# Empty rows stored two steps later, off the scatters' path, and a shorter plan for each expert slot

## The chip, the cores and the metric

One core of a Trainium2 chip runs the whole program. The metric is device time in microseconds (us) of that core; the median of three runs of the kernel before is 650.07 us (649.31 to 651.37).

## The reference

Windowed attention feeds a mixture of experts (MoE). There are 8 batches, 8 heads, 576 positions and head width 64; the 4608 rows that come out have 512 columns and go through one of 8 experts each, with hidden width 1024.

```python
scores = scale * np.matmul(q, k.transpose(0, 1, 3, 2))
mask = (rel >= 0) & (rel < window)                 # window = 64
attn = softmax(np.where(mask, scores, -1e9))
x = (attn @ v).transpose(0, 2, 1, 3).reshape(N, 512)
logits = x @ w_gate + modality_bias[modality_id]
e_idx = np.argmax(logits, axis=1)
gate_w = softmax(logits)[np.arange(N), e_idx]
for e in range(E):
    mask = e_idx == e
    out[mask] = gate_w[mask, None] * (np.maximum(x[mask] @ w1[e], 0.0) @ w2[e])
```

## The kernel before, in words

**Attention steps.** The 4608 rows are 36 pairs of 64-row blocks, 128 rows each. The main loop runs over steps `s` from 0 to 39. In step `s` the program takes the scores and minima of pair `s` (`scores`, `minima`, `exps`), transposes the probabilities of pair `s-1` (`probs_t`; ACT copies them out of PSUM as `pT`, L622) and multiplies by the values of pair `s-2` (`values`, PE tile `av`, L639). `values` needs `ve`, a copy of the pair's value rows shifted by half a pair, made one step earlier in `swap_v`: its lower half by POOL (L515), its upper half by DVE (L514). The result `xa` (L647) is transposed and goes to the gate logits of pair `s-3` (L664). The order on every engine is the order in which the code is written: instructions of an engine wait for their inputs in line.

**Routing.** Every two pairs form a group `G`. In step `s = 2G+5` a small matmul counts, for each row, the rows before it with the same expert (`route2`); `route3` makes from it the row's place `idx` in a DRAM table `xs_scratch`, and two indirect DMAs on POOL (L740, "scatters", one for each pair) store the 514-word rows (x, gate, row number) there. `cnt`, the eight experts' counts so far, comes out of PSUM at L765 where it is needed. The routing operations of DVE wait in a list `routing`, other small table operations in a list `queue`; `tick(n)` issues up to n of them, first the routing's, and with `table=True` the queue's.

**Empty rows.** Each expert's rows in the table are filled up with empty rows, whose row number is out of range. The table's last 256 rows are such empty rows; they are stored from the tile `padrow` by one DMA on SP's queue (L1065, in the profile `xs_scratch<-xt`, 514 KB) at the end of step 4. A step's scatters start in step 5.

**Expert slots.** From step 12 (`FIRST`) on, PE's work of expert slots is mixed into the attention steps: a slot takes 256 rows of one expert, loads them (`load_slot`, tile `xt`, L205), and runs both layers with split weights (`first` L283, `second` L305). The weights of two experts, 0 and 1 of `sel2`, stay in SBUF; their pieces come from DRAM as `y` tiles (L100, L104) during the attention steps, POOL casts the high part (L111) before step 12, and DVE makes the low part (L118). Table `EARLY` lists ten groups `T` behind whose scatters a slot is planned. `plan` computes which rows the slot reads: the number of full 256-row tiles of the expert counted so far, less those used, at most one; if there is none, the empty rows. SP reads the row number into a register (L203) and issues the load. After the attention steps the remaining tiles are planned and run by PE alone.

```python
        n = per_expert(pl, nm + "_n", tiles_of(pl, nm + "_f", cnt, False, TP), xs_)   # 3 + 2 operations
        n = tt(pl, nm + "_av", n, used[-1][:, xs_], ALU.subtract)
        take = ts(pl, nm + "_take", n, 1.0, ALU.min)
        row = stt(pl, nm + "_first", used[-1][:, xs_], 2.0, base2[:, xs_], ALU.mult, ALU.add)
        row = tt(pl, nm + "_at", row, take, ALU.mult)
        rows = ts(tab, f"rows_{len(used)}", row, float(DUMMY), ALU.add, dtype=I32)
        # and one or two more for the new number of used tiles: 11 or 12 in all
```

The first plan (`T` = 2) is written at the end of step 9; its 12 operations are issued in step 10 (`table`), and step 11 fetches the slot.

## Time and profile before

| | |
|---|---|
| median of the runs | 650.07 us (649.31 to 651.37) |
| the profiled execution | 651.72 us, of which the span of instructions 649.9 us |
| PE (matmul) busy | 621.9 us, 96% of the span |
| DVE, ACT, POOL busy | 366.5, 298.9, 139.9 us |
| mean granted TensorE clock | 0.985 |
| DMA | 88.59 MB, mean 136 GB/s |

Busy shares are means over stages with different limits, so the stretches have to be read one by one: the start and the first twelve steps last until about 91 us, then attention steps and slots run together, and after about 360 us slots alone. In the profile a wait is put down to the instruction that ended last before it, which need not be the one that was waited for.

### The profile page before, as it was taken

The page shows a single profiled execution, that of the slowest core. Times are in us where ns is not written, and L with a number is a line of the kernel's source. Part 1 is how long each engine was busy: PE and PEld are TensorE (multiplying, and loading weights), DVE is VectorE, ACT ScalarE, POOL GpSimd, SP SyncE. Part 2 cuts the span into 40 slices and gives each one's busy share as a digit, 9 for nine tenths or more (in the row PEclk, how much of TensorE's full clock was granted, in tenths as well). Part 3 has the DMA queues.
Part 4 walks back from the last instruction along what each step waited for, and adds up shares of the span by engine and source line. Part 5 has one row for each costly group of instructions (what it writes and reads, how often), then busy time and mean ns, then how long its engine had stood idle before and what let it go on. Part 6 is the DMA issues. An engine that isn't in the chain of part 4 may idle for free. (4 is left out here: it accounts for less than half of the span.)

```text
span 649.9 us, 17274 instructions
## 1 busy us (share of the span) xinstructions
PE 621.9 (96%) x6508; PEld 558.9 (86%) x6509; DVE 366.5 (56%) x1487; ACT 298.9 (46%) x931; POOL 139.9 (22%) x322
## 2 busy tenths in 40 slices
PE   6887889999999999999999999999999999999996
PEld 4777778988898989888888989999899999989986
DVE  2975996777767775766654364122223634757611
ACT  3875866756565656555644111111113422555411
POOL 5313530222132122221322220011011101101102
PEclk9996989999999999999999999999999999999999
DMA  9989675766855755453322123511050642677300
GB/s 166 197 217 223 174 203 136 189 159 149 195 139 130 186 138 136 108 133 88 99 84 66 66 98 129 198 66 56 15 189 34 215 142 80 212 246 234 119 2 35
DMA packets 140965, 88.59 MB, mean 136 GB/s; under 512 B 118826, under 2 KB 118864, under 8 KB 140752
## 3 DMA queue, kind: packets, MB, share of 16 engines
q1 hardware_dynamic: 132192, 67.97, 41.8%
q0 software_dynamic: 5856, 18.92, 7.7%
q10 hardware_dynamic: 2832, 0.59, 0.7%
q8 instruction: 52, 0.85, 0.6%
q14 instruction: 33, 0.27, 0.2%
HBM read 68.01 MB, written 23.91 MB: 141 GB/s over the span
## 5 line engine op out<-in xcount | busy, mean ns | idle before, releaser
L305 PE MATMUL y<-Whi,hh 128*128 128x512 f32 x288 | 118.7, 412 | 0.0
L305 PE MATMUL y<-Whi,hl 128*128 128x512 f32 x288 | 113.0, 392 | 0.0
L305 PE MATMUL y<-Wlo,hh 128*128 128x512 f32 x288 | 112.7, 391 | 0.0
L283 PE MATMUL em<-xh,Whi 128*128 128x256 f32 x400 | 102.7, 291 | 1.0 <-DVE xl L195 1.0
L283 PE MATMUL em<-xh,Wlo 128*128 128x256 f32 x400 | 98.0, 279 | 0.0
L613 ACT ACTIVATE ss<-ss,mn 128x128 f32<-128x128 f32 x240 | 94.1, 398 | 4.1 <-DVE mn L601 4.1
L292 DVE SCALAR_TENSOR_TENSOR hl<-em,hh 128x512 fp32r<-128x512 f32 x50 | 34.5, 690 | 94.2 <-ACT hh L291 92.5
L316 POOL DMA_INDIRECT out_dram<-y,id x36 | 37.3, 1036 | 224.1 <-DVE y L313 144.9
L283 PEld LDWEIGHTS em<-xh,Whi 128*128 128x128 f32 x400 | 75.3, 188 | 2.2 <-DVE xl L195 1.3
L283 PEld LDWEIGHTS em<-xh,Wlo 128*128 128x128 f32 x400 | 75.4, 188 | 0.9
L291 ACT ACTIVATE hh<-em 128x512 fp32r<-128x512 f32 x50 | 29.6, 593 | 92.9 <-PE em L283 88.9
L622 ACT COPY pT<-tp 128x512 f32<-128x512 f32 x59 | 32.7, 589 | 75.6 <-PE tp L443 75.6
L305 PEld LDWEIGHTS y<-Whi,hl 128*128 128x128 f32 x288 | 54.0, 188 | 12.3
L601 DVE CUSTOM_DVE_ANT_0 ss<-sp,masks 128x128 f32<-128x128 f32 x240 | 53.6, 286 | 19.1 <-PE sp L584 18.7
L283 PE MATMUL em<-xl,Whi 128*128 128x256 f32 x400 | 63.0, 279 | 0.0
L305 PEld LDWEIGHTS y<-Wlo,hh 128*128 128x128 f32 x288 | 54.3, 189 | 7.2
L305 PEld LDWEIGHTS y<-Whi,hh 128*128 128x128 f32 x288 | 54.1, 188 | 7.4
L740 POOL DMA_INDIRECT xs_scratch<-xa,idx x36 | 36.2, 1007 | 88.9 <-DVE lm L683 26.0
L639 PEld LDWEIGHTS av<-ve,pT 128*64 128x64 f32 x576 | 37.8, 142 | 19.5 <-POOL ve L515 9.3
L283 PEld LDWEIGHTS em<-xl,Whi 128*128 128x128 f32 x400 | 53.7, 188 | 0.0
L639 PE MATMUL av<-ve,pT 128*64 128x64 f32 x576 | 42.8, 230 | 10.0 <-POOL ve L515 6.3
L292 DVE SCALAR_TENSOR_TENSOR hl<-sp,hh 128x512 fp32r<-128x512 f32 x22 | 15.2, 691 | 61.1 <-ACT hh L291 61.1
(261 smaller groups left out, 1298.0 us busy)
## 6 DMA issues: line engine op xcount, KB each, us to landing
xt<-xs_scratch SPq DMA_DIRECT2D x18, 514.0 KB, 3.9
y<-in_moe_w_dram SPq DMA_DIRECT2D x32, 256.0 KB, 4.2
vo<-in_v_dram SPq DMA_DIRECT2D x27, 256.0 KB, 3.0
vo<-in_moe_w_dram SPq DMA_DIRECT2D x24, 256.0 KB, 4.0
ss<-in_moe_w_dram SPq DMA_DIRECT2D x24, 256.0 KB, 3.6
xs_scratch<-xs_scratch SPq DMA_DIRECT2D x8, 514.0 KB, 5.6
qk<-in_q_dram SPq DMA_DIRECT2D x16, 256.0 KB, 4.9
qk<-in_k_dram SPq DMA_DIRECT2D x16, 256.0 KB, 5.9
```

The source lines that it names most:

```text
L283: nc.tensor.matmul(out=hb[:, i * TP:(i + 1) * TP], lhsT=w[buf][:, c0:c0 + P], rhs=x[:, c * TP:(c + 1) * TP], start=(n == 0), stop=(n == le ...
L291: nc.scalar.activation(out=hh, in_=hb, func=AF.Relu),
L292: nc.vector.scalar_tensor_tensor(out=hl, in0=hb, scalar=0.0, in1=hh.bitcast(F32), op0=ALU.max, op1=ALU.subtract)))
L305: nc.tensor.matmul(out=sl["y", t], lhsT=h[:, i * TP + t * P:i * TP + (t + 1) * P], rhs=w[buf][:, c0:c0 + DM], start=(k == 0 and n == 0), s ...
L316: ins = nc.gpsimd.indirect_dma_start(out=out, out_offset=bass.IndirectOffsetOnAxis(ap=sl["id"][:, t:t + 1], axis=0), in_=y, in_offset=None ...
L601: nc.vector.tensor_tensor_reduce(out=ss[a][:, hp, :], in0=sp[a][:, hp * P:(hp + 1) * P], in1=mask, scale=-1.0 / 8.0, scalar=3.0e38, op0=AL ...
L613: nc.scalar.activation(out=ss[a][:, hp, :], in_=ss[a][:, hp, :], func=AF.Exp, bias=mn[:, h:h + 1], scale=-1.0, accum_out=sm[:, h:h + 1])
L622: nc.scalar.copy(out=pT, in_=pp)
L639: nc.tensor.matmul(out=av[c * W64:(c + 1) * W64, 2 * hp + a], lhsT=pT[:, i:i + W64], rhs=(vo if c else ve)[p][:, 2 * hp + a, :], start=Tru ...
L740: ins = nc.gpsimd.indirect_dma_start(out=xs, out_offset=bass.IndirectOffsetOnAxis(ap=idx[:, j:j + 1], axis=0), in_=xg[j], in_offset=None)
```

## The change

1. The store of the empty rows moves from the end of step 4 to the end of step 6, and is declared free of the scatters (their rows are never the same).
2. The plan of a slot keeps running numbers for each of the two experts: `used2`, `row2` (the expert's next row, in place of `base2`) and `room2` (the count from which a further full tile is there, 256 at first). A slot is taken where the expert's count is at least `room2`, so the counts need not be turned into tiles. 8 operations of DVE stand where 11 or 12 stood; four of them (five where two slots are planned) lead to the row number, the others carry the numbers on. A slot waits for the former alone (`need`).
3. The plan is written right behind the counts, ahead of `route3`, not at the end of the step. For the first plan (step 9) six operations are issued there at once; `table` for step 10 is gone.

```diff
+        n = per_expert(pl, nm + "_n", cnt, xs_)
+        used, row, room = used2[:, xs_], row2[:, xs_], room2[:, xs_]
+        one = xs_.stop - xs_.start < 2
+        if one:
+            at = stt(pl, nm + "_at", n, room, row, ALU.is_ge, ALU.mult)
+        else:
+            take = tt(pl, nm + "_take", n, room, ALU.is_ge)
+            at = tt(pl, nm + "_at", row, take, ALU.mult)
+        rows = ts(tab, f"rows_{len(todo)}_{T}", at, float(DUMMY), ALU.add, dtype=I32)
+        need = queued()
+        if one:
+            take = tt(pl, nm + "_take", n, room, ALU.is_ge)
+        tt(pl, nm, used, take, ALU.add, out=used)
+        stt(pl, nm, take, 2.0, row, ALU.mult, ALU.add, out=row)
+        stt(pl, nm, take, float(TP), room, ALU.mult, ALU.add, out=room)
...
-        table = s == FIRST - 2
...
-        tick(6 if table else 2, table)
+        tick(2)
...
-        tick(8 if table else n_tick, table)
+        tick(n_tick)
...
                 cnt = counts_out(tab if R == NG - 1 else pl, counts(R, tp))
+            for T, xs_ in EARLY:
+                if T == R:
+                    plan(T, xs_, cnt)
+                    tick(6 if s < FIRST else 0, table=True)
             route3(R, rk)
...
-        if s == 4:
-            nc.sync.dma_start(out=xs_blk[DUMMY:DUMMY + 2].rearrange("b p c -> p b c"), in_=padrow)
-        for T, xs_ in EARLY:
-            if T == R:
-                plan(T, xs_, cnt)
+        if s == 6:
+            ins = nc.sync.dma_start(out=xs_blk[DUMMY:DUMMY + 2].rearrange("b p c -> p b c"), in_=padrow)
+            tc.declare_no_dep(ins.ins, group="scatter", reason="rows behind every token's row")
+            tc.add_to_no_dep_group("scatter", ins.ins)
```

Three places of the built programs show what moved. POOL in step 5, at the first two scatters (`xa<-idc` writes the row numbers; the names in brackets are what the instruction waits for, DMAHW being DMAs of SP's queue):

```order
 L628 TENSOR_SCALAR rs<-sm 128x8 [waits DVE_49,Activation_49]
 L739 COPY xa_101<-idc 128x1
-L740 DMA xs_scratch<-xa_101,idx 39168x514 [waits DMAHW1_49,DVE_49,Pool_49]
+L740 DMA xs_scratch<-xa_101,idx 39168x514 [waits DVE_49,Pool_49]
 L739 COPY xa_102<-idc 128x1
 L740 DMA xs_scratch<-xa_102,idx 39168x514 [waits Pool_49]
```

The first scatter no longer waits for the DMA of the empty rows; nothing else on POOL moved. SP's queue in steps 4 to 7, before (`y` are weight pieces, `vo` values, the `Wlo` tiles hold q and k of later groups):

```order
L100 DMA y<-in_moe_w_dram 128x512
L1065 DMA xs_scratch<-xt 128x2x514
L536 DMA Wlo_65<-in_k_dram 128x8x64 x2
L100 ISA
L100 DMA y<-in_moe_w_dram 128x512
L501 DMA vo<-in_v_dram 128x8x64
```

and after, from the last piece of step 6 on:

```order
L104 ISA
L104 DMA y<-in_moe_w_dram 128x512
L1070 DMA xs_scratch<-xt 128x2x514
L501 DMA vo<-in_v_dram 128x8x64
L536 DMA Wlo_65<-in_k_dram 96x8x64 x2
```

The store goes past two weight pieces, one value load and six loads of k and q, and now stands ahead of the values of pair 7. DVE in step 10 before, behind the upper half of `ve` (the last of the 12 operations, `e_used`, follows):

```order
L514 COPY ve<-vo 64x512
L141 TENSOR_SCALAR e_f_i<-cnt 1x8
L165 TENSOR_SCALAR e_f_s<-e_f_i 1x8
L141 TENSOR_SCALAR e_f<-e_f_s 1x8
L153 TENSOR_TENSOR e_n_p<-sel_68,e_f 1x8
L158 TENSOR_REDUCE e_n<-e_n_p 1x1
L153 TENSOR_TENSOR e_av<-e_n,used_216 1x1
L550 COPY kT<-em 128x2x2x128
L141 TENSOR_SCALAR e_take<-e_av 1x1
L147 SCALAR_TENSOR_TENSOR e_first<-used_216,base_69 1x1
L153 TENSOR_TENSOR e_at<-e_first,e_take 1x1
L141 TENSOR_SCALAR rows_1495<-e_at 1x1
```

and DVE in step 9 after, behind the counts:

```order
L765 COPY cnt<-tp 1x8
L153 TENSOR_TENSOR e_n_p<-sel_68,cnt 1x8
L158 TENSOR_REDUCE e_n<-e_n_p 1x1
L147 SCALAR_TENSOR_TENSOR e_at<-e_n,room_226,row_69 1x1
L141 TENSOR_SCALAR rows_2_1462<-e_at 1x1
L153 TENSOR_TENSOR e_take<-e_n,room_226 1x1
L153 TENSOR_TENSOR used_216<-used_216,e_take 1x1
L721 TENSOR_TENSOR tgt<-tp,ebase 128x16
```

Six operations of the plan now stand ahead of the routing of step 9 (`tgt` is its first operation), and two, for `row2` and `room2`, behind the routing of step 10.

## The prediction

> **What bounds the kernel now.** I read the busy times by stretches first (columns: stretch, its length, busy us and instructions of PE, weight loads, DVE, ACT, POOL, then granted clock, DMA share, GB/s), and then PE's waits.

> ```profile
> 42.00:66.00 24.00, 18.25 (x280) 16.82 (x281) 14.53 (x70) 14.75 (x59) 8.19 (x15) 0.72 0.97 230
> 66.00:92.00 26.00, 21.73 (x415) 19.58 (x411) 24.32 (x131) 20.98 (x83) 11.13 (x21) 0.93 0.72 192
> 112.00:330.00 218.00, 216.33 (x2843) 194.89 (x2838) 151.27 (x732) 127.71 (x449) 53.66 (x110) 1.00 0.57 142
> 330.00:640.00 310.00, 309.50 (x2196) 279.37 (x2195) 133.15 (x333) 93.03 (x188) 44.06 (x97) 1.00 0.35 117
> ...
> PE av L639 <- POOL ve L515: 5.8, 2, 3.6
> ...
> PE em L443 <- DVE xa L647: 1.9, 1, 1.9
> PE av L639 <- DVE e_f_i L141: 1.2, 1, 1.2
> ```

> From 112 us on PE is full (216.33 of 218, 309.50 of 310), with the DMA engines half busy: what is lost or won before 112 us shifts everything behind it, and nothing there can take it up. Before that no engine is full. From 42 to 66 us PE waits 5.8 us for POOL's `ve` and its clock is 0.72; from 66 to 92 us DVE is busy 24.32 of 26. The change touches both places.

> Third, POOL's timeline at the first scatters, with the rows of SP, DVE and PE that belong to it (start, length, what, and in brackets the idle time before):

> ```profile
> 43.98 0.61 POOL L515 COPY ve<-Wlo 64x512 f32<-64x512 f32 x1
> 45.28 0.19 POOL L739 COPY xa<-idc 128x1 f32<-128x1 f32 x1
> 50.94 1.21 POOL L740 DMA_INDIRECT xs_scratch<-xa,idx  x1 [5.47 <-DVE lg L684]
> 52.17 0.19 POOL L739 COPY xa<-idc 128x1 f32<-128x1 f32 x1
> 52.64 0.96 POOL L740 DMA_INDIRECT xs_scratch<-xa,idx  x1 [0.28 <-POOL xa L739]
> 53.60 0.63 POOL L111 CAST Whi<-y 128x512 fp32r<-128x512 f32 x1
> 54.15 0.62 POOL L515 COPY ve<-Wlo 64x512 f32<-64x512 f32 x1
> ...
> 44.98 0.43 SPq L1065 DMA_DIRECT2D xs_scratch<-xt  x1
> ...
> 43.35 0.15 DVE L752 CAST idx<-dst 128x2 int32<-128x2 f32 x1
> 50.67 0.18 DVE L684 TENSOR_TENSOR lg<-lg,lm 128x16 f32<-128x16 f32 x1
> ...
> 50.66 0.60 PE L443 MATMUL em<-ident_r,Whi 128*128 128x128 f32 x4
> 54.83 0.37 PE L639 MATMUL av<-ve,pT 128*64 128x64 f32 x1 [3.57 <-POOL ve L515]
> ```

> The scatter's places `idx` are ready at 43.50 us (43.35 + 0.15), its row numbers at 45.47; it starts at 50.94. The profile names DVE `lg` only because that ended last before; the scatter does not read it. What it waits for is the empty rows' DMA, issued at 44.98. Behind it in POOL's line stand the second scatter, a weight cast and the `ve` that PE needs at 51.26 (50.66 + 0.60): PE stands until 54.83.

> Fourth, the clock in the same places (stretches cut where it changes), and ACT's first `pT` copy of each of steps 6 to 9, the beat of the steps:

> ```profile
> 43.08:46.49 3.41, 1.85 (x59) 1.83 (x62) 2.29 (x9) 3.16 (x14) 1.91 (x4) 1.00 1.04 250
> 46.49:49.91 3.42, 3.42 (x42) 3.09 (x35) 1.96 (x18) 0.59 (x2) 0.00 (x0) 0.50 1.10 286
> 49.91:53.32 3.41, 1.35 (x12) 1.12 (x10) 2.14 (x10) 3.41 (x16) 2.08 (x3) 1.00 0.99 235
> 53.32:63.56 10.24, 8.73 (x102) 8.32 (x103) 4.77 (x22) 4.07 (x16) 3.62 (x8) 0.50 1.11 244
> ...
> 49.05 0.59 ACT L622 COPY pT<-y 128x512 f32<-128x512 f32 x1 [2.81 <-PE y L443]
> 49.91 0.59 ACT L622 COPY pT<-y 128x512 f32<-128x512 f32 x1 [0.27 <-PE y L443]
> 60.56 0.59 ACT L622 COPY pT<-y 128x512 f32<-128x512 f32 x1 [5.91 <-PE y L443]
> 67.06 0.59 ACT L622 COPY pT<-tp 128x512 f32<-128x512 f32 x1 [0.97 <-PE tp L443]
> 72.61 0.59 ACT L622 COPY pT<-em 128x512 f32<-128x512 f32 x1 [0.31 <-PE em L443]
> ```

> A stretch in which PE works little (1.85 or 1.35 of 3.41 us) is followed by half clock: once for 3.42 us, and behind the long stall for 10.24 us. So the stall is paid twice. The steps show it: 11.51 us (49.05 to 60.56), 6.50, then 5.55.

> **The change, part by part.**

> *Scatter without the empty rows.* With idx and row numbers there at 45.47, the first scatter starts about 0.28 us later (as the second does), at 45.75 to 46.3 if the first pays some dispatch. Two scatters, copy and cast take the 3.26 us from 50.94 to about 54.2 as before, so `ve` is ready at 49.6 to 50.2 us, ahead of PE's 51.26. PE then runs on; its other input `pT` is there at 50.5 (49.91 + 0.59, the second copy of that step). The stretch from 49.91 has work throughout, so the half clock from 53.32 goes too. The steps 6 to 8 then take 5.55 us each, as the next one does: the copy at 67.06 comes at 49.05 + 2 x 5.55 = 60.15. **Gain 6.9 us**: 3.57 idle, 3.3 clock. The half clock from 46.49 stays, since its cause (a `ve` that waits for a weight piece) is not touched. Ends: 3.6 if only the idle goes; 8.6 if the other half-clock stretch (3.42 us, half of it lost) went as well.

> *The empty rows' DMA in step 6.* One issue (0.43 us) leaves SP's line at 44.98 and enters it ahead of the values of pair 7:

> ```profile
> 55.67 0.42 SPq L501 DMA_DIRECT2D vo<-in_v_dram  x1
> vo<-in_v_dram SPq DMA_DIRECT2D x1, 256.0 KB, 5.3
> ...
> 65.42 1.07 POOL L740 DMA_INDIRECT xs_scratch<-xa,idx  x1 [8.19 <-DVE rs L645]
> 68.49 0.83 POOL L515 COPY ve<-vo 64x512 f32<-64x512 f32 x1
> ```

> These values land at 55.67 + 5.3 = 61.0. The bytes issued ahead of them are the same in sum, only in another order, so I leave that at 61.0. POOL copies them behind two scatters at 68.49, after the change at 68.49 - 6.9 = 61.6. That hides the DMA with 0.6 us to spare: cost 0; the other end is in the rivals. Its rows are read first by the slot load of step 11, which does wait for it.

> *The plan on DVE.* The rows of step 9 and 10 (the third is ordinary work between, the row of e_n_p gives min, median, max in ns):

> ```profile
> 80.66 0.46 DVE L141 TENSOR_SCALAR e_f_i<-cnt 1x8 int32<-1x8 f32 x1
> 82.59 0.67 DVE L550 COPY kT<-em 128x512 f32<-128x512 f32 x1
> 83.19 0.13 DVE L141 TENSOR_SCALAR e_take<-e_av 1x1 f32<-1x1 f32 x1
> 83.43 0.15 DVE L153 TENSOR_TENSOR e_at<-e_first,e_take 1x1 f32<-1x1 f32 x1
> 83.94 0.15 DVE L683 TENSOR_REDUCE lm<-lg 128x2 f32<-128x16 f32 x1
> ...
> L153 DVE TENSOR_TENSOR e_n_p<-sel,e_f x10: 154/156/573, 81.5 to 357.4; 1x8 f32<-1x8 f32 x7, 1x16 f32<-1x16 f32 x3
> ...
> 85.94 0.69 DVE L647 TENSOR_TENSOR xa<-av,rs 128x512 f32<-128x512 f32 x1
> 86.69 0.66 PE L443 MATMUL em<-ident_r,xa 128*128 128x128 f32 x4 [1.91 <-DVE xa L647]
> ```

> Out go 82.59 - 80.66 = 1.93 and 83.94 - 83.19 = 0.75, together 2.68 us. In come six operations that mostly wait for one another, at about 0.18 us each (83.43 stands 0.24 behind e_take with one between): 1.05 us, and two at 0.12: 0.25. Net 1.4 us less on an engine that is full there. Against it, e_n_p took 573 ns here and 156 in the median, while POOL copied; that excess may fall on whatever stands there next, and e_f_i's (0.46) too, so that as little as 0.5 is left. The six also push the scatters and `ve` of step 9 back by 1.05 us, and PE, which already waits 1.2 us there, would idle some 2.3 and may draw half clock; DVE, not PE, ends that stretch (PE waits 1.91 for `xa`), and cover for PE is about that 1.91. I take **0.9 us**, between ends of -0.5 (half clock reaches DVE's inputs) and 1.4. In the nine later plans three or four operations less each lie beside a full PE: 0, at most the 1.7 us that PE still idles from 112 to 330. SP's read of the row number comes earlier, but the slot load then waits for its scatters: 0. One more 1x2 memset on POOL in the idle start: 0.

> *Sum.* 651.72 (profiled execution: span 649.9 plus 1.82 around it) - 6.9 - 0.9 = 643.9. The median, 650.07, lies 1.65 below; taken from it the sum is 642.3. Half-clock stretches of other lengths in other executions could be that difference, and then part of the term is not there to win. I take **643.2 us**.

> **The rivals.**

> *One half-clock stretch only.* If a stall of this size usually costs one stretch of 3.42 us, the clock part is 1.7, not 3.3: 650.07 - 3.6 - 1.7 - 0.9 = 643.9, or 645.5 on the profiled execution; about 644.7. For it: the first stall (PE 1.85 busy of 3.41) cost one. Against: the second cost 10.24 us. [...]

> *DMA becomes the bound.* Shares times lengths from 42 to 92 us: 24 x 0.97 + 26 x 0.72 = 42.0 us of transfer in 50; in 42.2 us they would fill the engines, which held 1.11 at most for 10 us. If late values or keys give back half the step term: 650.07 - 3.4 - 0.9 = 645.8, on the profiled execution 647.4; about 646.6. Against: loads run two to three steps ahead.

> *It does not do what it says.* Were the scatter really released by DVE `lg` (50.67 + 0.18, 0.09 us before its start), or by a slow first descriptor, only the plan's 0.9 is left: 649.2, no difference. For: the profile's own label. Against: that operand is not read.

> *Slower: the store's new place.* If the 514 KB delay the values of pair 7 by their full time, 45.0 to 50.9 = 5.9 us, they land at 66.9; `ve` is ready at 67.7 instead of 62.4, PE stands 5.3 us, and at the price of the old stall (6.9 for 3.6) that costs 10.2: 650.07 - 7.8 + 10.2 = 652.5. It decides from 4 us of lateness on. Against: the same bytes stood ahead of those values before. [...]

> **How the numbers follow.** A difference under 0.3% (2 us) of this kernel can't be told from none. Chances: the sum 0.58 (643.2; its own range 640.1 to 646.5, from terms 8.6 + 1.4 and 3.6 + 0), one stretch 0.12 (644.7), DMA 0.14 (646.6), nothing 0.10 (649.2), slower 0.06 (652.5). Faster: 0.58 + 0.12 + 0.14 = 0.84; same 0.10; slower 0.06. The range 640.5 to 647.5 holds the first three.

> **What would show it.** In the profile after: the first scatter within 1 us of its row numbers; no wait of PE for `ve` in step 7; clock 1.00 from about 50 us on; the `pT` copies of steps 7 and 8 each 5.5 to 5.7 us behind the last; POOL's `ve` of pair 7 not waiting for its values; DVE's `xa` of step 11 a further 0.9 us earlier; PE full from about 104 us. Wrong would make it: a wait of `values` for a DMA between 50 and 70, a half-clock stretch where none was, or a first scatter that starts as late as before.

## The result and the profile after

| | before | after |
|---|---|---|
| median of the runs, four each | 650.11 us (649.31 to 651.37) | 642.90 us (642.07 to 643.54) |
| ratio | | 0.9887 [0.9867, 0.9906] |
| the profiled execution, its span | 651.72, 649.9 us | 642.07, 640.3 us |
| mean granted clock | 0.985 | 0.998 |

The change saves 7.2 us by the medians. The two profiles lie 9.65 us apart, because the one before lies above all four runs of its kernel and the one after is the fastest of its own.

First the busy times by stretches, columns as in the prediction:

```profile
42.00:66.00 24.00, 19.96 (x406) 18.12 (x405) 21.45 (x107) 20.96 (x83) 12.02 (x21) 1.00 1.10 265
66.00:92.00 26.00, 21.83 (x403) 19.88 (x404) 23.45 (x121) 22.77 (x87) 11.97 (x23) 1.00 0.88 222
112.00:330.00 218.00, 216.98 (x2867) 195.62 (x2867) 145.30 (x701) 127.42 (x450) 55.11 (x114) 1.00 0.55 138
```

In 42 to 66 us PE now issues 406 matmuls where it issued 280, at full clock (1.00, it was 0.72). The DMA engines have become fuller (a share of 1.10, it was 0.97). From 112 us on PE is as full as before (216.98 of 218 us, it was 216.33).

PE's waits from 38 to 120 us (us in total, times, longest):

```profile
PE av L639 <- DVE lg L684: 2.3, 2, 1.7
PE av L639 <- POOL ve L515: 1.7, 1, 1.7
PE em L283 <- DVE xl L195: 1.2, 1, 1.2
PE y L711 <- issue: 1.2, 1, 1.2
PE av L639 <- POOL rs L628: 0.8, 2, 0.5
```

Of the 5.8 us for `ve` the larger wait (3.57) is gone and the first one (2.18 before, 1.73 now) is left. The 1.91 us for `xa` are gone too. New are 1.2 us before a routing matmul (L711), and 2.3 us that are put down to DVE's `lg`, of which more below.

The timeline at the first scatters (POOL, then PE's first matmuls of the values of steps 6 and 7):

```profile
45.52 0.19 POOL L739 COPY xa<-idc 128x1 f32<-128x1 f32 x1
46.02 1.21 POOL L740 DMA_INDIRECT xs_scratch<-xa,idx  x1 [0.30 <-POOL xa L739]
49.23 0.62 POOL L515 COPY ve<-Wlo 64x512 f32<-64x512 f32 x1
...
44.81 0.27 PE L639 MATMUL av<-ve,pT 128*64 128x64 f32 x1 [1.73 <-POOL ve L515]
50.28 0.24 PE L639 MATMUL av<-ve,pT 128*64 128x64 f32 x1 [0.46 <-POOL rs L628]
```

The scatter starts 0.31 us behind its row numbers (45.52 + 0.19), where it stood 5.47 us. PE's values of step 7 wait 0.46 us, it was 3.57. The label `rs` is again only what ended last: these matmuls read `ve`, of which POOL's half was ready at 49.85 and DVE's half at 50.14.

The clock in the stretches that the prediction shows (their edges are where the clock changed in the profile before, and mean nothing in this one), and ACT's first `pT` copies of steps 6 to 9:

```profile
43.08:46.49 3.41, 1.68 (x52) 1.66 (x56) 2.88 (x12) 3.41 (x15) 2.47 (x5) 1.00 1.01 259
46.49:49.91 3.42, 3.33 (x52) 2.92 (x52) 2.57 (x19) 2.17 (x8) 3.06 (x5) 1.00 1.17 297
...
53.32:63.56 10.24, 8.40 (x164) 7.58 (x163) 9.51 (x55) 8.83 (x36) 5.55 (x10) 1.00 1.09 248
```

```profile
48.11 1.07 ACT L622 COPY pT<-y 128x512 f32<-128x512 f32 x2 [1.25 <-PE y L443]
53.52 0.59 ACT L622 COPY pT<-y 128x512 f32<-128x512 f32 x1
59.92 0.59 ACT L622 COPY pT<-tp 128x512 f32<-128x512 f32 x1 [1.26 <-PE tp L443]
65.54 0.59 ACT L622 COPY pT<-em 128x512 f32<-128x512 f32 x1 [0.38 <-PE em L443]
```

No half clock is left there. The beats are 5.41, 6.40 and 5.62 us, where they were 11.51, 6.50 and 5.55.

The store and the values of pair 7 (SP's queue, the DMA from issue to landing, POOL's copy), and then the plan: DVE's first and last of its six operations and the `xa` behind it, POOL's `ve` of the values of step 11, and PE:

```profile
54.23 0.88 SPq L1070 DMA_DIRECT2D xs_scratch<-xt  x1
55.17 0.45 SPq L501 DMA_DIRECT2D vo<-in_v_dram  x1
...
vo<-in_v_dram SPq DMA_DIRECT2D x1, 256.0 KB, 5.6
...
61.37 0.89 POOL L515 COPY ve<-vo 64x512 f32<-64x512 f32 x1
```

```profile
68.43 0.15 DVE L153 TENSOR_TENSOR e_n_p<-sel,cnt 1x8 f32<-1x8 f32 x1
69.29 0.15 DVE L153 TENSOR_TENSOR used<-used,e_take 1x1 f32<-1x1 f32 x1
70.94 0.69 DVE L647 TENSOR_TENSOR xa<-av,rs 128x512 f32<-128x512 f32 x1
...
74.00 0.82 POOL L515 COPY ve<-vo 64x512 f32<-64x512 f32 x1
...
67.76 0.24 PE L639 MATMUL av<-ve,pT 128*64 128x64 f32 x1 [0.38 <-POOL rs L628]
74.87 0.27 PE L639 MATMUL av<-ve,pT 128*64 128x64 f32 x1 [1.66 <-DVE lg L684]
80.59 0.24 PE L639 MATMUL av<-ve,pT 128*64 128x64 f32 x1 [0.66 <-DVE ve L514]
```

The values of pair 7 land at 55.17 + 5.6 = 60.8 and are copied at 61.37, without a wait. PE's 1.66 us before the values of step 11 end with POOL's `ve` (74.00 + 0.82 = 74.82): that is the chain that the plan, now ahead of the scatters, pushes back.

**A measure for the stages.** All kernels below are compared by PE's first values matmul (L639) of a step: from step 6 to 10 lies the scatter's wait, from 10 to 12 the plan. Before, these stand at 44.64 (step 6), 74.97, 81.15 and 88.99 us (10, 11, 12); after, at 44.81, 67.76, 74.87 and 80.59. So 30.33 became 22.95 (7.38 less), and 14.02 became 12.83 (1.19 less). Of the 9.65 us the rest is 0.7 in step 12 (a half-clock stretch before at 87.5) and small pieces.

### The profile page after: what moved, and what is told of

The parts are those of the page before. It is cut to its first block, busy times and chain, and to the rows that moved or that the text cites. A ratio compares the mean times of both kernels' runs of the same rounds, so it can differ in the third digit from the quotient of the medians.

```text
span 640.3 us, 17239 instructions
## 1 busy us (share of the span) xinstructions
PE 615.6 (96%) x6508; PEld 552.9 (86%) x6509; DVE 359.7 (56%) x1449; ACT 298.8 (47%) x931; POOL 140.0 (22%) x323
## 4 chain that ended last, share of the span: by engine, by line
PE 50%; DVE 0%; ACT 0%; issue 0%; POOL 0%; POOLq 0%; ACTq 0%
PE y L305 23%; PE em L283 13%; PE sp L283 10%; PE tp L443 1%; PE y L356 1%; PE av L639 1%; PE em L258 1%; PE tp L258 1%; PE sp L331 0%; PE em L331 0%; PE tp L664 0%; PE sp L584 0%; DVE xa L647 0%; ACT ss L613 0%; POOL out_dram L369 0%
## 5 line engine op out<-in xcount | busy, mean ns | idle before, releaser
L622 ACT COPY pT<-tp 128x512 f32<-128x512 f32 x59 | 32.7, 590 | 76.4 <-PE tp L443 76.4
L601 DVE CUSTOM_DVE_ANT_0 ss<-sp,masks 128x128 f32<-128x128 f32 x240 | 53.6, 286 | 16.0 <-PE sp L584 15.7
L740 POOL DMA_INDIRECT xs_scratch<-xa,idx x36 | 36.2, 1006 | 74.3 <-DVE lm L683 26.1
L639 PEld LDWEIGHTS av<-ve,pT 128*64 128x64 f32 x576 | 36.3, 138 | 16.7 <-issue 7.5
L291 ACT ACTIVATE hh<-sp 128x512 fp32r<-128x512 f32 x22 | 13.2, 598 | 76.6 <-PE sp L283 76.6
## 6 DMA issues: line engine op xcount, KB each, us to landing
y<-in_moe_w_dram SPq DMA_DIRECT2D x32, 256.0 KB, 4.6
vo<-in_v_dram SPq DMA_DIRECT2D x27, 256.0 KB, 3.5
vo<-in_moe_w_dram SPq DMA_DIRECT2D x24, 256.0 KB, 3.6
ss<-in_moe_w_dram SPq DMA_DIRECT2D x24, 256.0 KB, 3.6
qk<-in_q_dram SPq DMA_DIRECT2D x16, 256.0 KB, 4.7
qk<-in_k_dram SPq DMA_DIRECT2D x16, 256.0 KB, 5.9
```

The lines of the kernel that those rows point to most:

```text
L291: nc.scalar.activation(out=hh, in_=hb, func=AF.Relu),
L601: nc.vector.tensor_tensor_reduce(out=ss[a][:, hp, :], in0=sp[a][:, hp * P:(hp + 1) * P], in1=mask, scale=-1.0 / 8.0, scalar=3.0e38, op0=AL ...
L622: nc.scalar.copy(out=pT, in_=pp)
L639: nc.tensor.matmul(out=av[c * W64:(c + 1) * W64, 2 * hp + a], lhsT=pT[:, i:i + W64], rhs=(vo if c else ve)[p][:, 2 * hp + a, :], start=Tru ...
L740: ins = nc.gpsimd.indirect_dma_start(out=xs, out_offset=bass.IndirectOffsetOnAxis(ap=idx[:, j:j + 1], axis=0), in_=xg[j], in_offset=None)
```

## The experiments

Each ratio is to the kernel before on the same chip; its median was 654.09, 655.97 and 653.60 us on the three chips used (first four kernels, the four from "The changed kernel again" on, the last four). The ratios are the recorded ones and differ by up to 0.0025 from the quotients of the medians. The times in the expectations of e1 to e4 were reckoned from the 650 us of the first runs, so on these chips only what a kernel saves can be compared. The lengths are those of the measure above, in the profiled execution; "half" is when the clock was halved before 125 us, and for how long.

| kernel | median us | ratio | steps 6 to 10 | 10 to 11, 11 to 12 | half |
|---|---|---|---|---|---|
| before | | | 30.33 | 6.18, 7.84 | 46.5 (3.4), 53.3 (10.2), 87.5 (3.4) |
| e1 store alone | 647.51 | 0.9915 [0.989, 0.994] | 23.86 | 6.35, 8.08 | none |
| e2 plan alone | 652.44 | 0.9983 [0.9962, 1.0004] | 29.52 | 7.11, 6.60 | 53.2 (6.8), 83.9, 97.5 (3.4 each) |
| e3 freed in step 4 | 649.39 | 0.9931 [0.9903, 0.9958] | 25.72 | 6.35, 8.11 | 59.0 (3.4) |
| e4 short plan, old place | 653.61 | 0.9996 [0.9971, 1.002] | 31.26 | 6.99, 6.91 | 53.6 (6.8), 70.7, 84.3, 98.0 (3.4 each) |
| the changed kernel again | 648.28 | 0.989 [0.987, 0.991] | 25.21 | 7.12, 5.72 | none |
| e5 cast later | 647.09 | 0.986 [0.9842, 0.9878] | 28.46 | 6.77, 5.70 | 63.8 (6.8), 91.1 (3.4) |
| e8 plan behind routing | 645.35 | 0.9827 [0.9812, 0.9842] | 24.48 | 6.35, 5.95 | 47.6, 91.9 (3.4 each) |
| e9 = e5 and e8 | 645.59 | 0.9848 [0.9829, 0.9867] | 24.26 | 6.37, 5.94 | 89.8 (3.4) |
| e6 second store in step 4 | 654.98 | 1.0025 [1.0012, 1.0037] | 31.43 | 6.35, 8.55 | 55.6 (6.8), 89.7 (3.4) |
| e7 second store in step 6 | 647.12 | 0.9921 [0.9896, 0.9946] | 23.48 | 7.12, 5.72 | none |
| e8 again | 645.74 | 0.9893 [0.9875, 0.9911] | 24.74 | 6.36, 5.95 | 46.9 (3.4) |
| e10 plan in step 10 | 646.16 | 0.991 [0.9887, 0.9933] | 23.71 | 6.36, 6.88 | 89.8 (3.4) |

**The store alone (e1).** The kernel before, with only the store moved to step 6 and freed:

```diff
-        if s == 4:
-            nc.sync.dma_start(out=xs_blk[DUMMY:DUMMY + 2]..., in_=padrow)
+        if s == 6:
+            ins = nc.sync.dma_start(out=xs_blk[DUMMY:DUMMY + 2]..., in_=padrow)
+            tc.declare_no_dep(ins.ins, group="scatter", ...)
+            tc.add_to_no_dep_group("scatter", ins.ins)
```

> The kernel before with the store of the empty rows alone moved to step 6 and freed from the scatters; the plan as before. Theory (PE stands behind POOL's first scatter, which waits for that store, and pays again in half clock): 643.5 to 645.5 us, the first scatter within 1 us of its row numbers, no wait of PE for ve in step 7, the pT copies of steps 6, 7 and 8 about 5.5 us apart. Rival (the shorter plan is what made the change faster): 649 to 650.5 us.

It is worth 0.85%, 5.5 us of 650 (3.9 to 7.2; 4.6 to 6.6 was expected), with no half clock before 125 us in its profile. The scatter starts 0.91 us behind its row numbers. The `pT` copies did not come 5.5 us apart but 5.15, 7.10 and 5.17. The plan's stage is about as long as before (14.43 us, it was 14.02), and DVE ends it:

```profile
69.43 0.24 PE L639 MATMUL av<-ve,pT 128*64 128x64 f32 x1 [0.40 <-DVE ve L514]
75.78 0.24 PE L639 MATMUL av<-ve,pT 128*64 128x64 f32 x1 [1.41 <-POOL rs L628]
81.56 0.65 PE L443 MATMUL em<-ident_r,xa 128*128 128x128 f32 x4 [2.15 <-DVE xa L647]
83.86 0.24 PE L639 MATMUL av<-ve,pT 128*64 128x64 f32 x1 [0.66 <-DVE ve L514]
```

**The plan alone (e2).** The changed kernel with the store back in step 4, as it was:

```diff
-        if s == 6:
-            ins = ...
+        if s == 4:
+            nc.sync.dma_start(out=xs_blk[DUMMY:DUMMY + 2]..., in_=padrow)
```

> The changed kernel with the store back in step 4 as before: the plan alone. Theory: 648 to 649.3 us (0.9 to 2 us less than before), the stall of 3 to 4 us before step 7 as in the kernel before, step 11 shorter by 1.5 to 3 us. Rival (the plan is the main part): under 646 us.

Its interval holds 1: no gain that the ratio can tell. The wait for the store is back, and longer than the 3 to 4 us expected (SP's store, POOL's first scatter, PE's values of step 7):

```profile
46.40 0.44 SPq L1070 DMA_DIRECT2D xs_scratch<-xt  x1
...
52.32 1.21 POOL L740 DMA_INDIRECT xs_scratch<-xa,idx  x1 [5.63 <-DVE oh L691]
...
56.20 0.37 PE L639 MATMUL av<-ve,pT 128*64 128x64 f32 x1 [5.55 <-POOL ve L515]
```

The scatter comes 5.92 us behind the store's issue, in the kernel before 5.96 (44.98 to 50.94); the instruction named is a different one (`oh`, `lg`), the distance the same.

**Freed, but left in step 4 (e3).** The store stays where it was and only gets the two lines that free it.

> The kernel before, the store left in step 4 but freed from the scatters; only the wait is gone, by the rows being distinct, as in the change. Theory (the wait): as e1_store within 0.7 us, 643.5 to 645.5 us. Rival (what helped is that the 514 KB left a stretch in which the DMA engines are full, and late loads were the stall): 648 us or more.

It has most of e1's gain, 4.5 us of 650 (2.7 to 6.3), and the intervals overlap: the wait is what counts, and a further gain from the place is not shown. Its one half-clock stretch follows the same odd idle time as in the changed kernel:

```profile
58.33 0.17 PE L711 MATMUL y<-oh,ones 128*128 128x8 bf16 x1 [1.80 <-issue]
```

**The short plan at the old place (e4).** The changed kernel with the store as before and `plan` written at the end of step 9, its operations issued in step 10.

> The kernel before with the short plan at its old place (8 operations in step 10, none in step 9), store as before. Theory: 12 operations of about 0.2 us become 8 in a stretch that DVE ends, so 649.0 to 649.5 us, 0.6 to 1.1 less than before, and less gain than e2_plan by 0.3 to 1 us. Rival (only the early place counts): no difference from before. Rival (the early place costs, since it holds back the scatters and ve of step 9): faster than e2_plan.

No difference from the kernel before, nor, with such intervals, from e2.

**The changed kernel again**, on the second chip.

> The changed kernel again, beside the three below on one chip. Theory: 0.989 of the kernel before (7 us less), the first pT copies of steps 5 to 8 each 5.4 to 5.7 us apart but for one beat of 6.4 between steps 7 and 8, where PE idles 1.2 us in the second routing matmul for no reason the profile shows; if that idle time is gone here, or elsewhere, it was chance of one execution.

The ratio repeats on another chip. The idle time at L711 repeats too (1.42 us), but its size is not fixed: in e10 it is 0.80 us and in both profiles of e8 it is missing, and these are the same program up to step 9.

**The first cast later (e5).** The changed kernel with POOL's first weight cast behind `ve` of step 5:

```diff
             sums(s - 1)
+            if s == 5:
+                weights(4)
...
-        if s >= 3:
+        if s >= 3 and s != 4:
             weights(s)
```

> The changed kernel with the first weight cast on POOL (and the load behind it) moved from the end of step 4 to step 5, behind that step's ve. Theory: the stall of the first ve, 1.7 us in the changed kernel, is a wait of the cast for its weight piece and goes: 1.0 to 2.2 us less than the changed kernel (some may come back, since the cast now stands ahead of the scatters and the next ve). Rival: the cast, waiting for the same late piece, holds up the scatters and the next ve by as much as it held up the first: no difference (within 0.5 us).

The first stall is gone, here and in e9, which has the same edit; so it comes from POOL's cast ahead of `ve`. But on this chip the changed kernel lost only 0.49 us by it: over the twelve profiles without this edit, whose programs are alike up to there, it is 0.49 to 4.30 us (e8), so the 1.7 of the expectation was one execution's. PE waits later, and 6.8 us of half clock follow:

```profile
49.46 0.27 PE L639 MATMUL av<-ve,pT 128*64 128x64 f32 x1 [1.43 <-DVE lg L684]
55.78 0.27 PE L639 MATMUL av<-ve,pT 128*64 128x64 f32 x1 [1.22 <-POOL ve L515]
63.05 0.24 PE L639 MATMUL av<-ve,pT 128*64 128x64 f32 x1 [2.34 <-POOL rs L628]
```

The times (1.2 us less by the medians, intervals that overlap) do not decide between theory and rival. The traces speak for the rival: in e9, without that half clock, the values of step 10 come 35.4 us behind those of step 4 (69.09 and 33.71), and without the edit, in e10, 35.5 (69.32 and 33.84).

**The first plan behind step 9's routing (e8, run on two chips), and with e5's edit (e9).**

```diff
                     plan(T, xs_, cnt)
-                    tick(6 if s < FIRST else 0, table=True)
             route3(R, rk)
...
         tick(n_tick)
+        if s == FIRST - 3:
+            tick(6, table=True)
```

> The changed kernel with the six operations of the first plan issued behind step 9's routing and not ahead of it. Theory of the prediction: ahead, they push the scatters and the ve of step 9 back by 0.9 us, and PE waits for that; behind, the beat of that step is 0.9 us shorter, and the whole is 0 to 0.8 us less if DVE does not end the stretch anyway. Rival: the early place is itself a gain, as the two kernels with the plan alone hinted (0.9983 early and short, 0.9996 short at the old place): behind, 0.5 to 1 us more.

> The kernel with the first plan behind step 9's routing once more, beside the next one. If its gain over the changed kernel is real: 0.981 to 0.985 of the kernel before; if it was chance: 0.987 to 0.990.

> Both edits together. If each is worth what its theory says: 1 to 3 us less than the changed kernel; if neither is, no difference.

On the second chip e8 was 2.9 us and e9 2.7 us below the changed kernel, with intervals apart. But the changed kernel ran only four times there, from 646.19 us at a granted clock of 0.999 to 650.24 at 0.986, and the mean clocks of its runs and e8's, 0.993 and 0.996, differ by what I estimate as up to 2.0 us of lost clock (0.003 of 648 us). On the third chip e8 had the ratio that the changed kernel has on the others. e9 gives no more than e8. So a gain in time over the changed kernel is not shown. In the traces a small one is, the same on both chips (steps 10, 11 and 12 of "e8 again"):

```profile
70.90 0.24 PE L639 MATMUL av<-ve,pT 128*64 128x64 f32 x1 [0.96 <-POOL rs L628]
77.26 0.24 PE L639 MATMUL av<-ve,pT 128*64 128x64 f32 x1 [0.88 <-POOL rs L628]
83.21 0.24 PE L639 MATMUL av<-ve,pT 128*64 128x64 f32 x1 [0.66 <-DVE ve L514]
```

6.36 + 5.95 = 12.31 us, the changed kernel 7.12 + 5.72 = 12.84.

**The first plan in step 10 (e10).** As e8, with `FIRST - 2`.

> As the one before, with the six operations of the first plan issued one step later, at the end of step 10. Theory: what cost time in the changed kernel was only that the six stood ahead of the scatters' places; anywhere behind them they are free: the same within 1 us. Rival: DVE is what ends step 10 to 11, and six operations there cost about 1 us, and the slot's load comes later: 1 to 2 us slower than the one before.

```profile
75.68 0.24 PE L639 MATMUL av<-ve,pT 128*64 128x64 f32 x1 [1.42 <-POOL rs L628]
80.26 0.66 PE L443 MATMUL em<-ident_r,xa 128*128 128x128 f32 x4 [0.95 <-DVE xa L647]
82.56 0.24 PE L639 MATMUL av<-ve,pT 128*64 128x64 f32 x1 [0.66 <-DVE ve L514]
```

Six operations in step 10 leave 0.95 us of the wait for `xa`, the old plan 2.15 (e1), none of it there 0. The stage takes 13.24 us, against 14.43 with the long plan there: the rival's mechanism is seen (0.9 us more than e8), though the times cannot tell it.

**A second store in step 4 (e6)**, to a table that nobody reads, ahead of the empty rows':

```diff
         if s == 4:
+            nc.sync.dma_start(out=pad2, in_=padrow)
             nc.sync.dma_start(out=xs_blk[DUMMY:DUMMY + 2]..., in_=padrow)
```

> The kernel before with a second store of 514 KB, to a table that nobody reads, ahead of the empty rows' in step 4. Theory of the prediction: the first scatter waits for the empty rows' DMA to land, so it starts later by the second store's transfer time; PE idles longer before the values of step 7 and loses about 1.9 us for each us of it (6.9 us for 3.57). With 2 to 4 us more of stall: 4 to 8 us slower than the kernel before (ratio 1.006 to 1.012). Rival: what the scatter waits for is not the landing (a DVE operation, or a first dispatch): no difference within 0.3%. Rival on the price: only idle time counts, 2 to 4 us (1.003 to 1.006).

```profile
46.53 0.43 SPq L1067 DMA_DIRECT2D xs_scratch<-xt  x1
...
54.28 1.21 POOL L741 DMA_INDIRECT xs_scratch<-xa,idx  x1 [7.33 <-DMA xs_scratch<-xt]
...
58.17 0.37 PE L640 MATMUL av<-ve,pT 128*64 128x64 f32 x1 [7.24 <-POOL ve L516]
```

The scatter now comes 7.75 us behind the store's issue, 1.8 more than before, and the profile names the store's DMA as what it waited for: the cause is shown. On the price the expectation failed. The kernel lost 1.6 us (0.8 to 2.4), about 0.9 for each us of delay and not 1.9, and its half clock behind the stall lasted 6.8 us, as in e2 and e4.

**A second store in step 6 (e7)**, the same edit in the changed kernel.

> The changed kernel with a second store of 514 KB, to a table that nobody reads, ahead of the empty rows' in step 6. Theory: the values of pair 7 have some us to spare in their new order, and nothing waits for the stores: within 2 us of the changed kernel (0.989 to 0.992 of the kernel before). Rival of the prediction (the store's new place delays the values): the values land 4 to 6 us later, PE stands for POOL's ve of pair 7 and the clock halves: 4 to 8 us slower than the changed kernel (0.995 to 1.002).

```profile
62.56 0.88 POOL L516 COPY ve<-vo 64x512 f32<-64x512 f32 x1 [0.24 <-DMA vo<-in_v_dram]
...
63.50 0.27 PE L640 MATMUL av<-ve,pT 128*64 128x64 f32 x1 [1.45 <-DVE lg L685]
```

POOL waits 0.24 us for the values of pair 7, and PE, which stands 1.45 us, starts 0.06 us behind POOL's `ve` (62.56 + 0.88), so it pays these 0.24. The rest of its wait is not the stores': e2, with the store in step 4, has 1.37 us in the same place. Nor is the 0.24 shown to be the second store's: e10 and e9, with one store, wait 0.40 and 0.28 there. The stage is 23.48 us long, no longer than without, and the ratio is at the upper end of the theory's, its interval below the rival's. The 4 to 6 us of lateness that the rival needs are not there.

## Why the prediction was right, step by step

- **What the scatter waits for.** Right: shown by e1 and e3 (wait gone), e2 (distance to the store kept) and e6 (DMA named, scatter later).
- **Its size.** 6.9 us was said; the two profiles differ by 7.38 from step 6 to 10, the three kernels that wait for one store take 30.4 us there on average, and six profiles with the store in step 6 and nothing else changed ahead of step 9 take 24.2 (22.95 to 25.21), so 6.2; in time e1 gives 5.5 (3.9 to 7.2). The working behind it was less right than the sum. Between the `pT` copies by which I reckoned, 18.01 us became 11.81, 6.2 less: a beat of 5.55 us for steps 6 to 8 did not come. The second was 6.40, with 1.16 us idle at L711 in it, and on the second chip PE's values of steps 7 to 9 came 6.66 and 6.88 us apart, with 1.42 idle there. The other 1.1 of the 7.38 us lie ahead of these copies and are luck: the half clock at 46.49, which I left standing, did not come in this execution, though its cause did. The signs were for one execution, too: on the second chip the first scatter started 1.47 us behind its row numbers, since `idx` came later there, and PE still waited 1.24 us before the values of step 7.
- **One half-clock stretch only (rival).** Half true: 10.24 us was one execution's; e2, e4 and e6 show 6.8. That may be why the median lost less than the profile, as the prediction's last step allowed; no run isolates it. The granted clocks on record allow an estimate: with one slope fitted to the times of the kernel before (23 runs) and of e1 (6) against the clock of each run (0.34 us for 0.001), e1 saves 3.5 us (2.6 to 4.4) at equal clock, and the other 2.6 of the 6.1 us between the means go with the clock. That is near the 3.57 us of idle time in the sum, and for the clock between the rival's 1.7 and the sum's 3.3.
- **The price of a stall.** 1.9 us for each us, on which the slower rival's 10.2 us rested, was mis-sized: e6 measured about 0.9. The half clock did not grow with the stall: it lasted 6.8 us behind 5.07, 5.55 and 7.24 us of idle time (e4, e2, e6).
- **The store in step 6 at no cost.** Nearly right: 60.8 to 61.37 is a margin of 0.6 us, as said, in the first profile, but it is no sure one. In e10 and e9, with the store in the same place, POOL waits 0.40 and 0.28 us for these values, and PE for POOL. The values stood directly behind the store in SP's queue, and still landed in 5.6 us (5.3 before). The slower rival, which needs 4 us, fails in e1 and in e7.
- **The plan, 0.9 us.** Mis-sized a little: its stage went from 14.43 us (e1) to 12.84 (the changed kernel on the second chip), 1.6 less, above my end of 1.4; in the first two profiles it was 1.19. The ratios (0.9915 and 0.989, intervals that overlap) can't tell. At equal clock, reckoned as for e1, the plan alone (e2) saves 1.3 us (0.6 to 2.0) and the short plan at its old place (e4) 0.6 (0.0 to 1.2), which fits the 0.9. The pieces are 1.2 for shortening (14.43 to 13.24) and 0.4 for the place. The cost of the place was seen rightly in kind (PE idles before the values of step 11, 1.66 us, for 2.3 said), but the cover was named wrongly: once the plan has left step 10, DVE no longer ends the stretch (`xa` is not waited for), so this wait is paid, and it is bought back only by the larger gain on `xa`.
- **DMA becomes the bound (rival).** Shares rose to 1.10, and POOL waits 3.3 and 3.4 us for values of other pairs, but PE was not held by these: its values of step 8 follow without a wait, and those of step 10 wait 0.38 us, to which DVE's half of `ve` (67.19 + 0.42) came last.
- **It does nothing (rival).** Fell.

## What to carry to other kernels

A wait in an engine's line is named after what ended last; measure the distance to each candidate's issue instead, and stretch one candidate to see whether the distance follows. Free an order that only a shared table imposes before moving the transfer, since here freeing alone gave most of it (4.5 us, e1 5.5). Work moved ahead of a chain is paid on that chain even if it disappears from the full engine (here PE's 1.66 us before the values of step 11): look for the place behind it.

## What the runs showed of the hardware

```profile
40.81:44.23 3.42, 2.27 (x23) 2.02 (x21) 3.33 (x21) 3.42 (x13) 0.66 (x2) 1.00 0.66 192
44.23:47.64 3.41, 2.83 (x82) 2.63 (x83) 2.11 (x8) 2.63 (x11) 2.74 (x5) 1.00 1.10 269
```

```profile
71.53:74.95 3.42, 1.61 (x14) 1.37 (x16) 3.32 (x22) 3.05 (x14) 3.04 (x6) 1.00 0.93 275
74.95:78.36 3.41, 3.41 (x89) 3.20 (x90) 3.22 (x12) 2.08 (x9) 2.23 (x5) 1.00 0.88 182
```

```profile
86.33:89.74 3.41, 1.64 (x14) 1.17 (x11) 2.82 (x18) 2.04 (x5) 3.26 (x7) 1.00 0.97 285
89.74:93.15 3.41, 3.11 (x14) 3.11 (x15) 3.27 (x11) 3.41 (x17) 0.16 (x1) 0.51 0.18 54
```

- With a second 514 KB store ahead of the first (e6) the scatter came 1.8 us later behind the issue, 7.75 us; with one alone it comes 5.96 behind (the kernel before) and 5.92 (e2).
- PE stood up to 1.80 us at L711 (e3; 1.16 and 1.42 in the changed kernel, 0.80 in e10, none in e8) with nothing named. What it waits for was not tried and stays open.
